# Spins in any idle bank, the first layer by weight block, weight sums at a later rank, two additions of the last tile on ScalarE and GpSimd

## The chip, the core and the metric

The program runs on one NeuronCore of a Trainium2 chip. The metric is the device time of one execution in microseconds, the median of three runs. The engines are TensorE (PE; its weight loads are listed as PEld), VectorE (DVE), ScalarE (ACT), GpSimd (POOL) and SyncE (SP), which issues nearly all DMA transfers.

## The reference

Attention with random features over 8 batches, 8 heads, 576 positions and 64 columns a head, and behind it a normalised two-layer network on the 4608 joined rows of 512:

```
proj = einsum('bhsd,md->bhsm', x, omega); h = proj - sum(x*x)/2
phi  = exp(h - max(h)) / sqrt(m)
kv = einsum('bhsm,bhsd->bhmd', phi(k), v); z = sum(phi(k))
attn = (phi(q) @ kv) / (phi(q) . z + 1e-6)
x   = attn as (B, S, H*D)
xn  = (x - mean) / sqrt(var + 1e-6) * g_ln
out = x + relu(xn @ w_ch1) @ w_ch2
```

`w_ch1` is 512 x 2048 and `w_ch2` 2048 x 512.

## The kernel before

The 4608 rows are nine tiles of 512 (`NT`), each of four chunks of 128 rows (`TC`). For each tile the kernel makes features of queries and keys, the sums `kv` of keys and values, the quotient `x`, its transposition `xnT`, the first layer (`mm1`, or `seven` from tile 2 on, with fewer products and more additions) and the second layer (`mm2`, or `deep` for the last two tiles). Float32 products are made of three products of a rounded high part and a low part.

The order on every engine is written by a planner in the kernel (`Plan`): each generator says which engine it will occupy and for how long by the planner's own figures, waits for keys (`wait`) or takes buffers and PSUM banks by name (`get`), and the planner picks what is ready first, by rank. PE, DVE, ACT, POOL and SP each execute their instructions in that order. Between engines, and from one tile to the next in the same buffer, the framework puts waits on semaphores: a new tile in a bank waits for the last writer and the readers of the tile before it.

In the first 39 us there is no layer to run yet. Chunks of keys are multiplied with `omega` (L909), DVE takes the maximum (L766), ACT the exponential (L784, or L772 on DVE and L778 on ACT for the chunks in `WIDE`), and PE multiplies with the values into `kv` (L827). Queries go through L957, a copy (L259 on ACT), a maximum over partitions on POOL (L1024), L1027 on DVE and L1032 on ACT; L1099 is their product with `kv`, L1111 to L1121 the quotient, L1148 and L1150 mean and variance, L1262 the centring, L1397 the transposition by PE, L1400 and L1402 its high and low part. Beside these, the weights are unpacked and split on DVE and ACT (L418 to L453; L446 is the last part of a first-layer block).

Times in which PE would have nothing are filled with spins (L370), matmuls of a constant of 256 columns that nobody reads. They all write one tile, `pw`, in the eighth bank, `banks[-1]`, which nothing else may use until the first layer starts. `gen_warm` issues them one by one at the rank for idle time, `sums` and `products` one after each group.

The first layer of tile 0 starts in `opening` for the four blocks of 128 columns `f` and for two halves `j` of the rows; it waits for the four weight blocks `w1_0` to `w1_3`, for two chunks of `xnT`, and runs `f` outside and `k` (the weight block) inside. `gen_sides` makes sums of first-layer weights that `seven` needs from tile 2 on. At the end, `combined` adds the partial sums of the last tile (L1847), and `quadrant` adds each quarter, scaled, to `x` (L1903) on DVE; when both quarters of a chunk are done, SP stores it (L1913).

## Time and profile before

| | us |
|---|---|
| median of 3 runs (909.53 to 909.95) | 909.66 |
| the profiled execution | 909.5 |
| its span, first to last instruction | 907.7 |
| PE busy | 902.0 |
| DVE busy | 777.1 |
| ACT busy | 543.2 |
| POOL busy | 138.2 |

The rows that are cited later come from four views. The page gives the busy time of each engine. The view by windows gives it for a stretch, with the count of instructions in brackets and the granted clock of TensorE. The timeline gives instructions in order of time: start, time, engine, line, operation, tile written and tiles read, count; in square brackets what the engine waited for ahead of it. A merged row of several instructions runs from the first one's start to the last one's end, so a step between two is the time less the length of one, divided by the count less one. The view by lines gives the mean length of one instruction. In the chain of waits a row is a stretch of the chain that ended last.

### The profile page before, as it was taken

To read this page: it belongs to the slowest core of one execution; us is meant where nothing else is said; L and a number is where in the kernel's file an instruction comes from. 1 tells how busy PE (TensorE), PEld (TensorE's weight loads), DVE (VectorE), ACT (ScalarE), POOL (GpSimd) and SP (SyncE) were. 2 spreads that over 40 slices of the span, in tenths; PEclk is the share of its full clock that TensorE was granted. 3 is DMA by queue.
4 is the path that set the end of the run, shared out by engine and by line. 5 is a ranking of instruction groups with operands and counts; after the bars stand their busy time and mean duration, and the time that the engine had idled before them with its cause. 6 is when DMAs were issued, how large, how long until landed. Compare 5 with 4: busy or idle time off the path is not lost.

```text
span 907.7 us, 21830 instructions
## 1 busy us (share of the span) xinstructions
PE 902.0 (99%) x8159; PEld 822.2 (91%) x8159; DVE 777.1 (86%) x1799; ACT 543.2 (60%) x1303; POOL 138.2 (15%) x107
## 2 busy tenths in 40 slices
PE   9999999999999999999999999999999999999998
PEld 7888788888899999998999999999999999999998
DVE  6999988989888899779898998888878788778767
ACT  7988876546566477546774666556555553453442
POOL 4201503300112042000220131002301400000000
PEclk9999999999999999999999999999999999999999
DMA  9199665558898898988999988889777869998981
GB/s 349 70 352 363 242 201 173 150 146 261 291 349 287 281 366 270 307 296 288 299 338 310 329 278 273 307 296 357 233 230 237 292 180 325 374 318 295 360 293 48
DMA packets 153146, 249.92 MB, mean 275 GB/s; under 512 B 13264, under 2 KB 66640, under 8 KB 153040
## 3 DMA queue, kind: packets, MB, share of 16 engines
q1 hardware_dynamic: 152752, 248.45, 81.2%
q8 instruction: 65, 1.06, 0.5%
q14 instruction: 41, 0.34, 0.1%
q10 hardware_dynamic: 288, 0.07, 0.0%
HBM read 205.47 MB, written 42.99 MB: 274 GB/s over the span
## 4 chain that ended last, share of the span: by engine, by line
PE 96%; DVE 2%; DMA 1%; ACT 0%; issue 0%; ACTq 0%; DVEq 0%
PE b L1421 38%; PE b L1510 29%; PE b L1794 7%; PE b L1759 6%; PE b L827 4%; PE b L1187 4%; PE b L865 2%; PE b L909 2%; PE b L1448 1%; PE b L370 1%; PE b L957 1%; PE b L1099 1%; DVE v L1847 0%; DVE kp L1903 0%; DMA hid<-omT 0%; DMA w<-side 0%
## 5 line engine op out<-in xcount | busy, mean ns | idle before, releaser
L1421 PE MATMUL b<-w,hid 128*128 128x512 f32 x1090 | 261.9, 385 | 0.0
L1421 PEld LDWEIGHTS b<-w,hid 128*128 128x128 f32 x1090 | 198.9, 188 | 34.0 <-issue 0.3
L1024 POOL PARTITION_ALL_REDUCE wide<-wide x72 | 134.8, 1893 | 473.8 <-ACT wide L259 271.4
L1510 PE MATMUL b<-xnT,w 128*128 128x256 f32 x1344 | 174.0, 276 | 0.0
L1510 PEld LDWEIGHTS b<-xnT,w 128*128 128x128 f32 x1344 | 164.3, 188 | 2.8
L1510 PE MATMUL b<-w,w 128*128 128x256 f32 x1008 | 126.1, 276 | 0.0
L1574 DVE TENSOR_TENSOR w<-b,w 128x256 f32<-128x256 f32 x224 | 108.7, 485 | 15.9 <-PE b L1510 10.4
L1510 PEld LDWEIGHTS b<-w,w 128*128 128x128 f32 x1008 | 120.5, 188 | 1.5 <-DVE w L1574 0.3
L880 ACT ACTIVATE kp<-kp,mb 128x128 f32<-128x128 f32 x184 | 66.9, 397 | 34.0 <-DVE mb L877 33.7
L1421 PE MATMUL b<-xnT,w 128*128 128x512 f32 x324 | 79.4, 387 | 0.0
L1421 PEld LDWEIGHTS b<-xnT,w 128*128 128x128 f32 x324 | 59.7, 187 | 12.0 <-issue 1.0
L1032 ACT ACTIVATE wide<-wide 128x512 f32<-128x512 f32 x72 | 45.4, 635 | 37.7 <-DVE wide L1027 37.7
L1759 PE MATMUL b<-w,hid 128*128 128x256 f32 x460 | 64.4, 279 | 0.0
L1759 PEld LDWEIGHTS b<-w,hid 128*128 128x128 f32 x460 | 57.6, 188 | 1.4
L1600 ACT ACTIVATE hid<-w 128x256 fp32r<-128x256 f32 x85 | 40.4, 513 | 30.4 <-DVE w L1574 24.7
L259 ACT COPY wide<-b 128x512 f32<-128x512 f32 x69 | 39.4, 586 | 28.5 <-PE b L1421 20.0
L1794 PE MATMUL b<-w,wide 128*128 128x256 f32 x408 | 52.4, 275 | 0.0
L1602 DVE SCALAR_TENSOR_TENSOR hid<-w,hid 128x256 fp32r<-128x256 f32 x85 | 48.3, 586 | 4.1 <-ACT hid L1600 3.3
L1027 DVE TENSOR_TENSOR wide<-wide,wide 128x512 f32<-128x512 f32 x64 | 47.0, 743 | 3.6 <-POOL wide L1024 3.4
L986 DVE TENSOR_TENSOR wide<-wide,wide 64x512 fp32r<-64x512 f32 x56 | 40.8, 734 | 9.7 <-ACT wide L984 8.2
L1794 PEld LDWEIGHTS b<-w,wide 128*128 128x128 f32 x408 | 49.1, 188 | 0.0
L886 ACT COPY kp<-b 128x256 f32<-128x256 f32 x92 | 31.4, 368 | 24.0 <-PE b L865 23.8
(171 smaller groups left out, 1453.6 us busy)
## 6 DMA issues: line engine op xcount, KB each, us to landing
w<-side SPq DMA_DIRECT2D x224, 256.0 KB, 5.0
w<-kept SPq DMA_DIRECT2D x80, 512.0 KB, 5.2
w<-kept SPq DMA_DIRECT2D x67, 256.0 KB, 5.2
w<-w SPq DMA_DIRECT2D x32, 512.0 KB, 7.2
wide<-qD SPq DMA_DIRECT2D x56, 256.0 KB, 5.3
w<-deep SPq DMA_DIRECT2D x47, 256.0 KB, 5.5
wide<-kD SPq DMA_DIRECT2D x40, 256.0 KB, 5.1
kept<-w SPq DMA_DIRECT2D x16, 512.0 KB, 3.9
```

The costliest lines, as they stand in the source:

```text
L880: nc.scalar.activation(out=kp[:, j], in_=kp[:, j], func=AF.Exp, scale=1.0, bias=mb[:, j : j + 1])
L986: nc.vector.tensor_tensor(out=qs[D:P], in0=qraw[D:P], in1=f32(qs[D:P]), op=ALU.subtract)
L1024: nc.gpsimd.partition_all_reduce(mx, qc, P, bass_isa.ReduceOp.max)
L1027: nc.vector.tensor_tensor(out=qc, in0=pq if direct else qc, in1=mx, op=ALU.subtract)
L1032: nc.scalar.activation(out=qc, in_=qc, func=AF.Exp)
L1421: nc.tensor.matmul(out.rearrange(f"p ({lies}) -> {order}", a=AW, b=BW), lhsT, rhs.rearrange(f"p (a c b) -> {order}", a=AW, b=BW), start=st ...
L1510: nc.tensor.matmul(passes(out), left(k, l), passes(right[:, r, k]), start=start and k + l + r == 0, stop=k + r == 2, skip_group_check=True,)
L1574: nc.vector.tensor_tensor(out=out, in0=left, in1=right, op=ALU.add)
L1600: nc.scalar.activation(out=hl[:, 0, cols], in_=x, func=AF.Relu)
L1602: nc.vector.scalar_tensor_tensor(out=hl[:, 1, cols], in0=x, scalar=0.0, in1=f32(hl[:, 0, cols]), op0=ALU.max, op1=ALU.subtract)
L1759: nc.tensor.matmul(accs[i].rearrange("p (c a b) -> p c a b", a=AW, b=BW)[:, :, n * 8 : n * 8 + 8], hl[:, l, cs], w[:, r, n * HC : (n + 1) ...
L1794: nc.tensor.matmul(out.rearrange("p (c a b) -> p c a b", a=8, b=8), left[:, l, chunk * P : (chunk + 1) * P], right[:, r].rearrange("p (a c ...
```

## The change

`warm` no longer writes one tile: it takes, of all banks that the planner knows to be free by then, the one free longest, and makes a new tile in it; the eighth bank is no longer set aside. The copies of query features of the first two blocks may go to DVE too. `opening` waits for each weight block when it comes to it, and for the first half of the rows runs `k` outside and `f` inside; `mm1` waits block by block too. In the last tile, the quarter `n == 1` of chunks 2 and 3 is scaled on ACT and added on GpSimd. The rank of the weight sums grows by 12 a group where it grew by 1. Of the two wide chunks of keys, the second is now chunk 3. Since the planner works from these figures, the order of many instructions in the layers differs.

```
-    pw = tile_of(banks[-1], [P, 512], F32, ps)[:, 0 : 2 * P]
-
-    def warm(n):
-        if not mlp_on:
+    def warm(n, at=0.0):
+        idle = [] if mlp_on else [x for x in banks if plan.places.get(x, 1e9) <= plan.cur.end - at]
+        if n and idle:
+            to = bank(min(idle, key=plan.places.get), 2 * P)
             for _ in range(n):
-                nc.tensor.matmul(pw, spin[:, 0:P], spin, start=True, stop=True)
+                nc.tensor.matmul(to, spin[:, 0:P], spin, start=True, stop=True)
...
-        eng = yield "run", {ACT: 0.48, DVE: 0.62} if blk >= T // QB else {ACT: 0.58}
+        eng = yield "run", {ACT: 0.48, DVE: 0.62} if blk >= T // QB else {ACT: 0.58, DVE: 0.62}
...
-        for k in range(NK):
-            yield wait("w", 1, k)
...
-            for f in range(count):
+            places = [(k, f) for k in range(NK) for f in range(count)]
+            for k, f in places if j == 0 else sorted(places, key=lambda x: x[1]):
                 if j == 0:
+                    yield wait("w", 1, k)
+                if j == k == 0:
...
     def mm1(t, f):
-        for k in range(NK):
-            yield wait("w", 1, f // NK * NK + k)
...
         for k in range(NK):
+            yield wait("w", 1, f // NK * NK + k)
             yield us(PE, 3 * 0.225)
...
+        acc = acc.rearrange("p (c r) -> p c r", r=P // 2)
+        if t == NT - 1 and i >= 2 and n == 1:
+            yield act(HC)
+            nc.scalar.activation(out=acc, in_=acc, func=AF.Copy, scale=rss[:, c : c + 1])
+            yield us(POOL, 0.8)
+            nc.gpsimd.tensor_tensor(out=half, in0=acc, in1=half, op=ALU.add)
+        else:
+            yield dve(HC)
...
     def gen_warm():
-        plan.places.pop(banks[-1])
         plan.cur.after = 1.0
         while not mlp_on:
             cold = plan.cur.end < COLD
-            yield us(PE, 0.29 if cold else 0.11)
-            warm(1)
+            cost = 0.29 if cold else 0.11
+            yield us(PE, cost)
+            warm(1, cost)
             plan.cur.after = plan.cur.end + (0.0 if cold else WARM)
-        free(banks[-1])
...
-            plan.add(RSIDE + g, gen_sides(g, k))
+            plan.add(RSIDE + 12 * g, gen_sides(g, k))
...
-WIDE = ((0, 0), (0, 2))
+WIDE = ((0, 0), (0, 3))
```

On PE, at the start of the program, in the kernel before: the last two of thirteen spins and the first product of keys (`om`). A name is a bank, `b0` to `b7`, with the number of the tile in it; the words in brackets are the semaphores that the instruction waits for.

```order
L370 LDWEIGHTS spin_74
L370 MATMUL b7_93<-spin_74 128x256
L370 LDWEIGHTS spin_74
L370 MATMUL b7_93<-spin_74 128x256
L909 MATMUL b0_136<-om_86,w2_150_95 128x128 [waits DMAHW1_49,DVE_49]
L909 MATMUL b1_137<-om_86,w2_150_95 128x128
```

The same place on PE in the changed kernel.

```order
L370 MATMUL b0_135<-spin_74 128x256 [waits PE_49]
L370 LDWEIGHTS spin_74
L370 MATMUL b6_139<-spin_74 128x256
L370 LDWEIGHTS spin_74
L370 MATMUL b6_141<-spin_74 128x256 [waits PE_49]
L370 LDWEIGHTS spin_74
L370 MATMUL b6_143<-spin_74 128x256 [waits PE_49]
L370 LDWEIGHTS spin_74
L370 MATMUL b6_145<-spin_74 128x256 [waits PE_49]
L909 MATMUL b0_148<-om_86,w2_150_94 128x128 [waits DMAHW1_49,DVE_49]
L909 MATMUL b1_149<-om_86,w2_150_94 128x128
```

Spins that shared one tile now have a tile each, and each that takes the bank of the spin before it waits for PE's own semaphore. The program has 101 spins before and 64 now; 45 of the 64 wait for the matmul directly ahead of them.

On PE, where the first layer starts, in the kernel before: the last of ten spins, the third transposition (`ident`), and the first layer (`xnT`, `w1_0` with the number 369, `w1_1`).

```order
L370 LDWEIGHTS spin_74
L370 MATMUL b7_93<-spin_74 128x256
L1397 MATMUL b5_712<-ident_76,wide10_693 128x128 [waits PE_49,Activation_49]
L1397 MATMUL b5_712<-ident_76,wide10_693 128x128 x3
L1448 MATMUL b6_710<-xnT0_624,w1_00_369 128x4x8x8 [waits DVE_49,PE_49]
L1448 MATMUL b6_710<-xnT0_624,w1_00_369 128x4x8x8
L1448 MATMUL b6_710<-xnT0_624,w1_00_369 128x4x8x8 [waits DVE_49]
L1448 MATMUL b6_710<-xnT0_624,w1_10_493 128x4x8x8 x3
```

The same place in the changed kernel, behind nine spins.

```order
L370 MATMUL b6_719<-spin_74 128x256 [waits PE_49]
L370 LDWEIGHTS spin_74
L370 MATMUL b6_721<-spin_74 128x256 [waits PE_49]
L1448 MATMUL b6_724<-xnT0_627,w1_00_452 128x4x8x8 [waits PE_49,Activation_49]
L1448 MATMUL b6_724<-xnT0_627,w1_00_452 128x4x8x8
L1448 MATMUL b6_724<-xnT0_627,w1_00_452 128x4x8x8 [waits DVE_49]
L1448 MATMUL b4_734<-xnT0_627,w1_00_452 128x4x8x8 x3
L1448 MATMUL b2_739<-xnT0_627,w1_00_452 128x4x8x8 x3
L1448 MATMUL b3_743<-xnT0_627,w1_00_452 128x4x8x8 x3
L1448 MATMUL b6_724<-xnT0_627,w1_10_517 128x4x8x8 x3
```

The third transposition has moved behind the first two weight blocks, and the first block now serves four banks in a row. Ahead of this place the spin groups of 17, 10 and 10 have become 18, 8 and 9.

On DVE, at the end of the program, in the kernel before: the last sums (L1847) and the additions to `x` (`kp`, L1903).

```order
L1847 TENSOR_TENSOR v2_12379<-v0_12378,b4_11555 128x512 [waits DVE_49]
L1847 TENSOR_TENSOR v0_12378<-v0_12378,b0_11536 128x512 [waits DVE_49]
L1903 SCALAR_TENSOR_TENSOR kp1_9416<-v2_12379,rss_83,kp1_9416 128x4x64
L1847 TENSOR_TENSOR v1_12380<-v1_12380,b7_11611 128x512 [waits PE_49]
L1903 SCALAR_TENSOR_TENSOR kp1_9416<-v2_12379,rss_83,kp1_9416 128x4x64
L1903 SCALAR_TENSOR_TENSOR kp1_9416<-v0_12378,rss_83,kp1_9416 128x4x64 [waits DVE_49]
L1903 SCALAR_TENSOR_TENSOR kp1_9416<-v0_12378,rss_83,kp1_9416 128x4x64
L1903 SCALAR_TENSOR_TENSOR kp0_9415<-b3_3342,rss_83,kp0_9415 128x4x64 [waits PE_49]
L1903 SCALAR_TENSOR_TENSOR kp0_9415<-v1_12380,rss_83,kp0_9415 128x4x64 [waits DVE_49]
L1903 SCALAR_TENSOR_TENSOR kp0_9415<-v1_12380,rss_83,kp0_9415 128x4x64
L1903 SCALAR_TENSOR_TENSOR kp0_9415<-b2_3343,rss_83,kp0_9415 128x4x64 [waits PE_49]
```

The same place on DVE in the changed kernel.

```order
L1846 TENSOR_TENSOR v2_12462<-v0_12461,b4_11638 128x512 [waits DVE_49]
L1846 TENSOR_TENSOR v0_12461<-v0_12461,b0_11619 128x512 [waits DVE_49]
L1846 TENSOR_TENSOR v1_12463<-v1_12463,b7_11694 128x512 [waits PE_49]
L1909 SCALAR_TENSOR_TENSOR kp1_9499<-v0_12461,rss_83,kp1_9499 128x4x64 [waits DVE_49]
L1909 SCALAR_TENSOR_TENSOR kp1_9499<-v0_12461,rss_83,kp1_9499 128x4x64
L1909 SCALAR_TENSOR_TENSOR kp0_9498<-b2_3475,rss_83,kp0_9498 128x4x64 [waits PE_49]
L1909 SCALAR_TENSOR_TENSOR kp0_9498<-v1_12463,rss_83,kp0_9498 128x4x64 [waits DVE_49]
L1909 SCALAR_TENSOR_TENSOR kp0_9498<-v1_12463,rss_83,kp0_9498 128x4x64
L1909 SCALAR_TENSOR_TENSOR kp0_9498<-b3_3476,rss_83,kp0_9498 128x4x64 [waits PE_49]
```

The two additions from `v2` have left DVE; they are the last two instructions on POOL, behind two scalings that are the last two on ACT. The stores on SP keep their order, chunks 2, 3, 0, 1, and the first two also wait for POOL.

## Rows read from the trace of the kernel before

**Rows 1.** The page, busy time, share and instructions of each engine.

```profile
PE 902.0 (99%) x8159; PEld 822.2 (91%) x8159; DVE 777.1 (86%) x1799; ACT 543.2 (60%) x1303; POOL 138.2 (15%) x107
```

**Rows 2.** Windows: stretch, us, busy of PE PEld DVE ACT POOL, PEclk, DMA, GB/s.

```profile
6.11:21.31 15.20, 15.11 (x235) 12.07 (x231) 13.86 (x31) 13.48 (x35) 9.28 (x6) 1.00 1.04 398
...
38.98:903.66 864.68, 864.58 (x7617) 792.62 (x7615) 744.47 (x1720) 512.73 (x1224) 122.28 (x91) 1.00 0.83 277
```

**Rows 3.** Timeline of the start: start, us, engine, line, operation, tiles, count, wait.

```profile
1.19 2.95 PE L370 MATMUL b<-spin 128*128 128x256 bf16 x13 [1.19 <-DVE spin L330]
...
4.22 1.66 PEld L909 LDWEIGHTS b<-om,w 64*128 64x128 f32 x16 [0.56 <-DVE om L376]
...
6.11 1.29 DVE L766 TENSOR_REDUCE mb<-b 128x4 f32<-128x512 f32 x2 [1.94 <-PE b L909]
```

**Rows 4.** By lines, until 4.1 us and from 9 to 38.3: busy us, mean ns.

```profile
L370 PE MATMUL b<-spin 128*128 128x256 bf16 x13 | 3.0, 419 | 1.2 <-DVE spin L330 1.2
...
L370 PE MATMUL b<-spin 128*128 128x256 bf16 x88 | 13.2, 275 | 0.0
```

**Rows 5.** Timeline of PE from the first L1099 to the first L1448.

```profile
26.95 0.69 PE L1099 MATMUL b<-kv,wide 128*64 128x65 f32 x16
...
30.06 2.03 PE L370 MATMUL b<-spin 128*128 128x256 bf16 x17
...
35.57 1.27 PE L370 MATMUL b<-spin 128*128 128x256 bf16 x10
...
37.11 1.25 PE L370 MATMUL b<-spin 128*128 128x256 bf16 x10
38.57 0.66 PE L1397 MATMUL b<-ident,wide 128*128 128x128 f32 x4 [0.21 <-ACT wide L1262]
38.98 2.64 PE L1448 MATMUL b<-xnT,w 128*128 128x256 f32 x21
```

**Rows 6.** Timeline of DVE, three neighbours late in the program.

```profile
892.87 0.43 DVE L1664 SCALAR_TENSOR_TENSOR kv<-w 128x256 f32<-128x256 f32 x1
893.33 0.43 DVE L1677 TENSOR_TENSOR kv<-kv 128x256 f32<-128x256 f32 x1
893.67 0.42 DVE L1602 SCALAR_TENSOR_TENSOR hid<-w,hid 128x256 fp32r<-128x256 f32 x1
```

**Rows 7.** Timeline of DVE and ACT around the last keys of the first batch.

```profile
18.11 0.68 DVE L434 SCALAR_TENSOR_TENSOR wide<-w 128x512 uint32<-128x512 uint32 x1
...
20.02 1.29 DVE L766 TENSOR_REDUCE mb<-b 128x4 f32<-128x512 f32 x2 [0.50 <-PE b L909]
...
20.74 2.17 ACT L784 ACTIVATE w<-b,mb 128x128 f32<-128x128 f32 x8 [0.43 <-DVE mb L766]
```

**Rows 8.** The chain of waits around 210 us: start, us, what.

```profile
210.37 25.11 PE b L1421 x114
...
250.71 2.73 PE b L1510 x24
```

**Rows 9.** Timeline of the last 11 us: DVE, PE and SP's queue.

```profile
897.15 3.63 DVE L1847 TENSOR_TENSOR v<-v,b 128x512 f32<-128x512 f32 x5
...
903.16 0.50 PE L1794 MATMUL b<-w,hid 128*128 128x256 f32 x3
903.27 0.87 DVE L1903 SCALAR_TENSOR_TENSOR kp<-v,rss,kp 128x256 f32<-128x256 f32 x2
904.06 0.48 DVE L1903 SCALAR_TENSOR_TENSOR kp<-b,rss,kp 128x256 f32<-128x256 f32 x1
```

**Rows 10.** Timeline of POOL, two reductions over partitions.

```profile
12.48 3.77 POOL L1024 PARTITION_ALL_REDUCE wide<-wide  x2 [1.28 <-ACT wide L259]
```

**Rows 11.** Timeline at the second group of first-layer blocks: DVE and PE.

```profile
57.93 0.75 DVE L446 SCALAR_TENSOR_TENSOR w<-wide,g_sb,w 128x512 fp32r<-128x512 f32 x1
...
58.38 2.80 PE L1421 MATMUL b<-xnT,w 128*128 128x512 f32 x12
```

More of the change, by code (lines that the diff above doesn't have):

```diff
@@ L1443, in opening @@
                 cs = slice(f % 2 * P, (f % 2 + 1) * P)
-                for k in range(NK):
-                    yield us(PE, 3 * 0.1134)
-                    w = wparts[1, k][:, f // 2]
-                    for l, r in ((0, 0), (1, 0), (0, 1)):
-                        nc.tensor.matmul(
-                            out, w[:, l, cs],
-                            passes(xnT[:, r, k])[:, :, 8 * j : 8 * j + 8],
-                            start=j + k + l + r == 0, stop=j == 1 and k == NK - 1 and r == 1, skip_group_check=True,
-                        )
-                if j == 1:
+                yield us(PE, 3 * 0.1134)
+                w = wparts[1, k][:, f // 2]
+                for l, r in ((0, 0), (1, 0), (0, 1)):
+                    nc.tensor.matmul(
+                        out, w[:, l, cs],
+                        passes(xnT[:, r, k])[:, :, 8 * j : 8 * j + 8],
+                        start=j + k + l + r == 0, stop=j == 1 and k == NK - 1 and r == 1, skip_group_check=True,
+                    )
+                if j == 1 and k == NK - 1:
                     done(("mm1", 0, f))
@@ L1459, in mm1 @@
     def mm1(t, f):
-        for k in range(NK):
-            yield wait("w", 1, f // NK * NK + k)
         for i in range(TC):
@@ L1900, in quadrant @@
             yield wait("part", t, i, None)
-        yield dve(HC)
         half = x.rearrange("p (c n r) -> p n c r", n=2, r=P // 2)[:, n or 0]
-        nc.vector.scalar_tensor_tensor(
-            out=half, in0=acc.rearrange("p (c r) -> p c r", r=P // 2), scalar=rss[:, c : c + 1], in1=half,
-            op0=ALU.mult, op1=ALU.add,
-        )
+        acc = acc.rearrange("p (c r) -> p c r", r=P // 2)
[6 more added lines that the diff above has]
+            yield dve(HC)
+            nc.vector.scalar_tensor_tensor(
+                out=half, in0=acc, scalar=rss[:, c : c + 1], in1=half, op0=ALU.mult, op1=ALU.add
+            )
         done(("part", t, i, n))
```

## The prediction

> **What bounds the kernel now.** I read the page first: PE is busy for 902.0 of 907.7 us [rows 1]. Then the windows: from the first layer's first matmul at 38.98 us to the last at 903.66 PE is busy for 864.58 of 864.68 us [rows 2], so no wait of PE worth naming is left there. For the same matmuls the end can only move with two things: when the first layer starts, and the tail from PE's last matmul to the last store, 907.7 - 903.66 = 4.0 us. The rest of the argument is about the first 39 us, where PE executes in program order, real products and spins (L370) mixed, each spin group filling a time in which data is made ready by DVE, ACT and GpSimd. The profiled execution took 909.5 us (span 907.7); the median of the three runs is 909.66, so I add the sum to 909.66.
>
> **What a spin costs, before and after.** The first thirteen spins take 2.95 us [rows 3] and last 0.419 us each [rows 4]: a step of (2.95 - 0.42)/12 = 0.211 us for 256 columns, the 1.2 GHz level. Later a spin lasts 0.275 us [rows 4], and seventeen take 2.03 us [rows 5]: a step of (2.03 - 0.28)/16 = 0.110 us, the 2.4 GHz level. Step is shorter than length because spins overlap: they all write one tile, b7, and none waits. In the changed order each spin gets a tile of its own, and one that lands in the bank of the spin just before it carries a wait on PE's own semaphore, which that spin raises at its end. I count 47 waits on the directly preceding matmul where the kernel before has none, 45 of them on spins. Such spins can't overlap: the step becomes length plus signal. No row shows this on PE. The nearest are on DVE [rows 6]: two neighbours without such a wait start 0.34 us apart (893.67 after 893.33), while the operation that waits for the one just before it starts 0.46 us after it, which is its length of 0.43 plus 0.03. So I take 0.275 + 0.03 = 0.305 us a spin, and 0.42 + 0.03 = 0.45 at the low clock. The lower end is the old 0.110, if the wait costs nothing.
>
> **The change, part by part.**
> (1) *First spins.* Thirteen stay, eleven with a wait. The thirteenth starts at 1.19 + 11 x 0.45 + 0.21 = 6.35 us and the first product of keys behind it at 6.56, where it now starts at 4.22, on om [rows 3]: +2.3 us, and the first reduction on DVE (6.11 now) goes with it. If the clock also rises later, two product groups cost up to half the 1.66 us of the first group's loads [rows 3] more each: bounds 0 and +4.0.
> (2) *Work up to the first L1099.* Eight banks instead of seven, the WIDE chunk moved, copies allowed on DVE. Between the first and the last of the ten reductions DVE has in the new order four weight operations fewer (L426, L430, L434, L267; at most 0.68 us each, [rows 7]) and one copy more: three fewer, at 0.4 to 0.68, about -1.6. DVE is busy for 13.86 of 15.20 us there [rows 2]; of the 1.34 us idle I give half back, -0.7. From the end of the last exponentials (20.74 + 2.17 = 22.91, [rows 7]) to the first L1099 at 26.95 [rows 5] 4.0 us pass, with twelve spins and a product of queries among the work; the new order has two L827 groups of about 0.63 us, five spins (4 x 0.305 + 0.11 = 1.33) and the copies of the sums: about 3.4, so -0.6. Together -2.9, bounds -1.2 and -4.8. With (1), the first L1099 comes at 26.95 + 2.3 - 2.9 = 26.35.
> (3) *From the first L1099 to the first L1448.* Now 38.98 - 26.95 = 12.03 us [rows 5]. The real products are the same but for the third transposition. The spin groups change: 17 at 0.11 = 1.9 become 18, sixteen of them waiting: 16 x 0.305 + 0.22 = 5.1 (+3.2). Ten, 1.1, become eight, six waiting: 2.05 (+0.95). Ten become nine, eight waiting: 2.55 (+1.45). Away go PE's wait in front of the third transposition (37.11 + 1.1 = 38.21 to 38.57, -0.36) and the transposition (38.57 to 38.98, -0.41). Sum +4.8; with a signal between nothing and 0.06 us, +3.9 to +5.7. I take the sum whole, because the data that these groups cover is ready before they end: a transposition's copy and the next centring on ACT are some 1.3 us, less than the new groups behind it.
> (4) *First layer by weight block.* Its 96 matmuls stay, in another order. It removes the wait for w1_3, whose last part now stands behind the second L1402 on DVE; I cost it at nothing, since PE arrives later than before. The third transposition returns inside it: +0.41.
> (5) *Weight sums put off, new order of the layers.* Same instructions on DVE and SP. PE has 43 matmuls of 512 columns fewer and 86 of 256 more: 86 x 2.73/24 - 43 x 25.11/114 = +0.3 [rows 8]. New waits: bounded by nothing and 1 us; I take nothing, because PE has none now [rows 2], and the weights get the time by which the layer starts later.
> (6) *The tail.* PE ends at 903.66 (903.16 + 0.50), but the last addition on DVE starts at 904.06, behind two others from 903.27 [rows 9]. Two quarter additions (some 0.4 us each) leave DVE, so the last starts at about 903.70: -0.36. Their scaling on ACT and addition on GpSimd begin when the fourth L1847 ends: 897.15 + 3 x 0.74 + 0.68 = 900.05. The stores wait on SP in order; the two of the chunks that GpSimd adds stand first, so a late GpSimd holds back the last store too. No row has a GpSimd addition; the nearest is its reduction over 128x512, 3.77/2 = 1.89 us [rows 10]: at that price the second addition ends at 900.05 + 0.5 + 3.8 = 904.3 and the last store is some 0.8 us later than now. Bounds -0.36 and +0.8; I take -0.36, since the operands here have half the elements and no exchange between partitions. The Trainium skill (GPSIMD Engine Reference, 3.1 Elementwise) has 4497 ns for an addition of 2048 elements; an estimate from it is 0.56 us here, which would leave -0.36 too.
>
> Sum: (1) +2.3, (2) -2.9, (3) +4.8, (4) +0.4, (5) +0.3, (6) -0.36 = +4.55. 909.66 + 4.55 = **914.2 us**. With the bounds of (1) to (3) partly offsetting each other: 911.5 to 917.
>
> **Rivals.**
> *A wait on PE's own semaphore costs nothing* (the spins keep 0.110). For: in-order PE has no need of the wait, and no row shows one that close. Against: [rows 6]. Then (1) is 0, (2) is -2.9 less another 0.8 for its five spins, (3) is +0.1 - 0.2 - 0.1 - 0.77 = -1.0; with (4) to (6) about -4.3. Of that something is given back: w1_7's last part is ready at 57.93 + 0.75 = 58.68 and needed about nine matmuls of 0.22 after 58.38, at 60.4 [rows 11], a margin of 1.7 us that such a start exceeds, so -2.0 to -4.3: **906.5 us**. This is the faster side. Where it tips: thirty waiting spins behind the first L1099, four ahead of it and eleven slow ones at the start make some 0.45 us for each 0.01 us of step, so from a step of about 0.20 us on the change is slower.
> *The clock falls.* Waiting spins occupy the array for 0.11 of each 0.305 us, for 5 us in the longest group; before that group nothing so thin is seen, and the granted clock is 1.00 in the rows of the windows [rows 2]. If it falls to 1.2 GHz, the fourteen waiting spins after it cost 0.145 more each (2.0 us) and up to 22 of the first layer's matmuls run at half rate (2.3 us): **917 to 918.5 us**. By the Trainium skill (TensorE: Matmul & The Clock Gate, A second HAM failure mode: psum-queue depth-cycling) PE that idles briefly and often while it cycles through banks can swing between its two clock levels; the row shows no such fall in the kernel before, which has no waits of that kind.
> *The spin groups do cost, but the front gains more* (all of DVE's idle time and the low end of (2) and (3)): **910.5 us**.
>
> **Chances.** Forecast 0.60, clock 0.12, smaller loss 0.08, free waits 0.20. The range leaves out the free waits alone: 909.5 to 918. A measurement of this kernel tells 0.2% (1.8 us) from no change: faster 0.18 (the free waits without their slow end), same 0.10 (that end and most of the smaller loss), slower 0.72.
>
> **What would show it.** In the changed kernel's profile: spins in a group of one bank 0.30 us apart (0.11 would prove me wrong at the root); the first L909 at 6.3 to 6.8 us and the first DVE reduction near 8; the first L1099 at 25.5 to 27.5; the first layer's first matmul at 42 to 45 us; PE again without waits from there to its end; the last addition on DVE within 0.1 us of PE's end. A first layer that starts before 38 us, or PE waits of more than 1 us in all behind it, would make the prediction wrong.

## The result, and the profile after

The changed kernel takes 920.39 us (median of six runs, 919.36 to 923.57) against 909.99 us: a ratio of 1.0119 (1.0103 to 1.0135). The forecast was 914.2 us, at most 918. The direction was right; the forecast growth (4.2 us over this median) is less than half of the measured 10.4 us.

The profiled execution is the longest of the six: 923.57 us, span 921.7 us, 14.0 us more than the span before (907.7). The span in four stretches, before and after:

| stretch | before, us | after, us | difference |
|---|---|---|---|
| start to first L1448 | 38.98 | 49.07 | +10.09 |
| first L1448 to first L1421 | 11.45 | 13.48 | +2.03 |
| first L1421 to PE's end | 853.23 | 855.48 | +2.25 |
| PE's end to the end of the span | 4.05 | 3.67 | -0.38 |

The timeline of PE after (start, time, engine, line, operation, tiles, count, and in brackets what PE waited for ahead of it):

```profile
1.17 5.30 PE L370 MATMUL b<-spin 128*128 128x256 bf16 x13 [1.17 <-DVE spin L330]
6.40 2.08 PE L909 MATMUL b<-om,w 64*128 64x128 f32 x16
8.27 1.92 PE L957 MATMUL b<-wide,om 64*128 64x256 f32 x8
...
12.58 1.03 PE L957 MATMUL b<-wide,om 64*128 64x256 f32 x8
...
19.64 1.16 PE L909 MATMUL b<-om,wide 64*128 64x128 f32 x14 [0.93 <-DVE w L727]
...
28.80 0.69 PE L1099 MATMUL b<-kv,wide 128*64 128x65 f32 x16
...
31.91 6.27 PE L370 MATMUL b<-spin 128*128 128x256 bf16 x18
38.11 1.14 PE L1099 MATMUL b<-kv,wide 128*64 128x65 f32 x16
...
43.43 2.34 PE L370 MATMUL b<-spin 128*128 128x256 bf16 x8
...
46.05 2.87 PE L370 MATMUL b<-spin 128*128 128x256 bf16 x9
49.07 4.57 PE L1448 MATMUL b<-xnT,w 128*128 128x256 f32 x24
...
62.55 5.47 PE L1421 MATMUL b<-w,hid 128*128 128x512 f32 x24
```

Read the spins first. Before, seventeen took 2.03 us [rows 5]; now eighteen take 6.27. The nine at 46.05 us take 2.87 us and the last of them lasts 0.28, so a step is (2.87 - 0.28)/8 = 0.324 us (0.325 below) where it was 0.110. Then read the products: L1099 behind the long group takes 1.14 us for sixteen, 0.69 ahead of it. PE itself is slower there. The windows of after (stretch, length, busy time and count of each engine, granted clock, DMA share, GB/s) say so in the clock's column:

```profile
31.91:35.58 3.67, 3.05 (x16) 1.14 (x13) 3.33 (x10) 3.67 (x16) 0.77 (x3) 1.00 0.00 0
35.58:42.41 6.83, 6.55 (x60) 4.09 (x60) 2.08 (x10) 1.77 (x3) 0.00 (x0) 0.50 0.01 2
42.41:49.23 6.82, 5.89 (x42) 2.96 (x41) 4.74 (x13) 5.01 (x17) 0.00 (x0) 1.00 0.00 0
49.23:52.65 3.42, 3.42 (x17) 3.42 (x17) 2.91 (x8) 2.17 (x4) 0.00 (x0) 0.50 0.00 0
...
62.55:918.03 855.48, 854.85 (x7559) 783.17 (x7557) 731.40 (x1704) 503.40 (x1215) 124.18 (x93) 1.00 0.84 279
```

The granted clock is at the lower of its two levels (1.2 GHz) from 35.58 to 42.41 us and again from 49.23 to 52.65, where the first layer begins. Before, it was 1.00 in [rows 2], and between them in the stretch from the first L1099 on:

```profile
26.95:38.98 12.03, 11.82 (x184) 9.65 (x184) 11.78 (x38) 11.16 (x32) 2.58 (x4) 1.00 0.01 3
```

At the very start the column reads 1.00 in both kernels, though the first spins of the kernel before step by 0.211 us and later ones by 0.110. That PE runs there at the lower level is read from the lengths alone: in the changed kernel eight L957 still take 1.92 us at 8.27 us, and 1.03 at 12.58.

The last row of after answers to the second of [rows 2]: in the layers behind the opening PE waits for 0.63 us (855.48 less 854.85) where it waited for 0.10 us before, but they are 2.25 us longer.

The tail went as forecast. DVE's last addition starts 0.10 us behind PE's end (918.03), where it was 0.40 us [rows 9]; ScalarE and GpSimd are done well before:

```profile
914.47 0.91 ACT L1904 ACTIVATE v<-v,rss 128x256 f32<-128x256 f32 x2 [3.77 <-DVE v L1846]
915.07 1.67 POOL L1906 TENSOR_TENSOR kp<-v,kp 128x256 f32<-128x256 f32 x2 [172.38 <-ACT v L1904]
...
918.13 0.47 DVE L1909 SCALAR_TENSOR_TENSOR kp<-b,rss,kp 128x256 f32<-128x256 f32 x1
```

### The profile page after: what moved, and what is told of

The parts are those of the page before. It is cut to its first block, busy times and chain, and to the rows that moved or that the text cites. A ratio compares the mean times of both kernels' runs of the same rounds, so it can differ in the third digit from the quotient of the medians.

```text
span 921.7 us, 21865 instructions
## 1 busy us (share of the span) xinstructions
PE 911.9 (99%) x8165; PEld 825.0 (90%) x8165; DVE 775.8 (84%) x1799; ACT 544.8 (59%) x1317; POOL 141.1 (15%) x109
## 4 chain that ended last, share of the span: by engine, by line
PE 91%; DVE 5%; DMA 2%; ACT 1%; issue 1%; DVEq 0%; SPq 0%
PE b L1421 35%; PE b L1509 28%; PE b L1793 7%; PE b L1758 6%; PE b L1187 4%; PE b L827 3%; PE b L865 2%; PE b L1448 1%; DMA w<-w 1%; PE b L370 1%; PE b L909 1%; PE b L1479 1%; PE b L1099 1%; DMA w<-kept 1%; DVE w L1573 0%
## 5 line engine op out<-in xcount | busy, mean ns | idle before, releaser
L1421 PE MATMUL b<-w,hid 128*128 128x512 f32 x1065 | 254.2, 384 | 0.0
L1421 PEld LDWEIGHTS b<-w,hid 128*128 128x128 f32 x1065 | 194.7, 188 | 33.3 <-issue 0.3
L1509 PEld LDWEIGHTS b<-xnT,w 128*128 128x128 f32 x1344 | 165.1, 188 | 3.3
L1421 PE MATMUL b<-xnT,w 128*128 128x512 f32 x306 | 76.5, 389 | 0.0
L1758 PE MATMUL b<-w,hid 128*128 128x256 f32 x510 | 69.6, 278 | 0.0
L1032 ACT ACTIVATE wide<-wide 128x512 f32<-128x512 f32 x72 | 45.8, 636 | 35.5 <-DVE wide L1027 34.0
L1421 PEld LDWEIGHTS b<-xnT,w 128*128 128x128 f32 x306 | 56.0, 187 | 11.4 <-issue 1.0
L1254 ACT ACTIVATE wide<-x,mvs 128x512 f32<-128x512 f32 x28 | 35.0, 1260 | 16.0 <-DVE mvs L1150 7.0
L986 DVE TENSOR_TENSOR wide<-wide,wide 64x512 fp32r<-64x512 f32 x56 | 38.6, 700 | 5.6 <-ACT wide L984 4.2
```

What stands on the lines that cost most here:

```text
L986: nc.vector.tensor_tensor(out=qs[D:P], in0=qraw[D:P], in1=f32(qs[D:P]), op=ALU.subtract)
L1032: nc.scalar.activation(out=qc, in_=qc, func=AF.Exp)
L1421: nc.tensor.matmul(out.rearrange(f"p ({lies}) -> {order}", a=AW, b=BW), lhsT, rhs.rearrange(f"p (a c b) -> {order}", a=AW, b=BW), start=st ...
L1509: nc.tensor.matmul(passes(out), left(k, l), passes(right[:, r, k]), start=start and k + l + r == 0, stop=k + r == 2, skip_group_check=True,)
L1758: nc.tensor.matmul(accs[i].rearrange("p (c a b) -> p c a b", a=AW, b=BW)[:, :, n * 8 : n * 8 + 8], hl[:, l, cs], w[:, r, n * HC : (n + 1) ...
```

## The experiments

Fourteen kernels, in three questions: is it the spins' waits, through what do they cost, and what do the other edits do? "Ratio" is always against the kernel before on the same chip. Line numbers of some kernels are shifted by up to six (L1453 or L1444 for L1448 and so on).

### Is it the waits?

The first kernel takes the changed one and lets spins share a tile as long as nothing else used the bank.

```
-            to = bank(min(idle, key=plan.places.get), 2 * P)
+            name = min(idle, key=plan.places.get)
+            if spun[0] != (name, plan.places[name]):
+                spun[:] = (name, plan.places[name]), bank(name, 2 * P)
+            to = spun[1]
```

> The changed kernel, and only the tiles of the spins differ: a spin takes the tile of the spin before it as long as it is in the same bank and nothing else used the bank in between, so none of the 64 spins waits for PE's own semaphore; the order on every engine is that of the changed kernel, row for row. Theory A (the waits of the spins, and the clock that they cost): the step of two spins goes from 0.325 us to 0.15 us, the first product of keys starts near 4.2 us, the clock is granted in full near 6 us instead of 11.7 us, no later stretch is at half of it, the first L1448 starts at 36 to 39 us (49.07 with the waits), and the time is 905 to 909 us. Theory B (the order of the other work, made by the planner, is what costs; the spins follow it): 916 to 921 us. Theory C (64 spins are too few where 101 stood before, waits or not): the clock still falls in the front, and the time is 910 to 916 us.

Measured: 911.59 us, ratio 1.0015 (1.0006 to 1.0024). The waits alone, with every row of the order the same, are worth 8.8 us of the 10.4 by the medians (9.4 by the ratios). Theory A holds, but the end is 2.6 us above its range: the front comes out as it said, the rest does not. Its timeline of PE:

```profile
1.17 2.96 PE L375 MATMUL b<-spin 128*128 128x256 bf16 x13 [1.17 <-DVE spin L330]
4.25 1.28 PE L914 MATMUL b<-om,w 64*128 64x128 f32 x16
...
10.38 0.69 PE L832 MATMUL b<-w,kp 128*64 128x65 f32 x16 [0.95 <-ACT kp L789]
...
16.90 1.16 PE L914 MATMUL b<-om,wide 64*128 64x128 f32 x14 [0.93 <-DVE w L732]
...
25.20 0.69 PE L1104 MATMUL b<-kv,wide 128*64 128x65 f32 x16
...
28.31 1.48 PE L375 MATMUL b<-spin 128*128 128x256 bf16 x12
30.29 0.81 PE L375 MATMUL b<-spin 128*128 128x256 bf16 x6 [0.49 <-DVE wide L1032]
...
36.16 1.15 PE L375 MATMUL b<-spin 128*128 128x256 bf16 x9
37.46 3.06 PE L1453 MATMUL b<-xnT,w 128*128 128x256 f32 x24
```

Nine spins take 1.15 us again, a step of (1.15 - 0.28)/8 = 0.109 us. The first L1448 (here L1453) starts at 37.46 us, 11.6 us ahead of the changed kernel.

The second does the reverse: the kernel before, with a tile for each call of the spins.

```
-    pw = tile_of(banks[-1], [P, 512], F32, ps)[:, 0 : 2 * P]
...
+            pw = bank(banks[-1], 2 * P)
```

> The kernel before, and only the tiles of the spins differ: each call of the spins makes a tile of its own in the reserved eighth bank, so nearly every one of the 101 spins waits for the matmul ahead of it; the order on every engine stays that of the kernel before. Theory A (waits and clock): the first product of keys starts near 6.4 us (4.22 without), the clock is granted in full later than 5.7 us, the first L1448 starts at 43 to 50 us (38.98 without), and the time is 914 to 921 us. Theory B (the order costs, not the waits): the waits are hidden, 909 to 911 us. Between them, 911 to 914 us, the waits would cost their own length in the front and the clock nothing.

Measured: 929.00 us, ratio 1.0205 (1.0191 to 1.0219), 8 us beyond the range of theory A. Not a row of the order differs, so 19 us are the price of the waits on PE's own semaphore, with what the clock loses by them:

```profile
1.19 5.52 PE L369 MATMUL b<-spin 128*128 128x256 bf16 x13 [1.19 <-DVE spin L330]
6.64 2.08 PE L908 MATMUL b<-om,w 64*128 64x128 f32 x16
...
41.35 5.51 PE L369 MATMUL b<-spin 128*128 128x256 bf16 x17
46.79 0.95 PE L1098 MATMUL b<-kv,wide 128*64 128x65 f32 x16
...
58.62 2.65 PE L1447 MATMUL b<-xnT,w 128*128 128x256 f32 x21
```

The seventeen spins take 5.51 us, (5.51 - 0.28)/16 = 0.327 us a step, where they took 2.03; 0.217 us more each. At 1.2 GHz the first thirteen step by (5.52 - 0.42)/12 = 0.425 us against 0.211 before [rows 3]. There are 86 spins in seven groups of ten and more, so 79 such steps; 79 x 0.217 = 17.1 us. The front is 58.62 - 38.98 = 19.6 us longer. The rest fits two stretches with a low clock:

```profile
30.30:33.59 3.29, 3.29 (x42) 2.18 (x42) 0.46 (x1) 1.07 (x2) 0.50 (x1) 0.53 0.00 0
46.79:50.46 3.67, 3.67 (x52) 2.86 (x51) 2.21 (x8) 0.93 (x4) 0.00 (x0) 0.54 0.02 4
```

The same instructions took 1.91 us (22.78 to 24.69) and 2.40 us (32.02 to 34.42) before, 2.65 us less. Behind the first L1421 the two are alike, 853.12 us (70.04 to 923.16) against 853.23.

The third undoes the spins' edit and keeps all others; the planner makes a new order.

```
-    def warm(n, at=0.0):
-        idle = [] if mlp_on else [x for x in banks if plan.places.get(x, 1e9) <= plan.cur.end - at]
...
+    pw = tile_of(banks[-1], [P, 512], F32, ps)[:, 0 : 2 * P]
```

> The changed kernel with the first of its edits undone: the spins write one tile in the eighth bank again, which is set aside until the first layer starts (109 spins, none with a wait on PE). All other edits stay, and the planner makes its order anew. Theory A (waits and clock of the spins): within 3 us of the kernel before, 906 to 911 us. Theory B (the other edits, by the order that they make): 915 to 921 us.

Measured: 912.87 us, ratio 1.0032 (1.0020 to 1.0044). Far nearer to A's 906 to 911 than to B's 915 to 921, but 1.9 us above: the other edits cost some 3 us without the waits.

### Which waits, and through what?

Each spin in the next idle bank in turn, so that it waits for a matmul two or more back:

```
-            to = bank(min(idle, key=plan.places.get), 2 * P)
+            spun[0] += 1
+            to = bank(idle[spun[0] % len(idle)], 2 * P)
```

> The changed kernel, and only the banks of the spins differ: each spin makes a tile of its own as there, but in the next of the idle banks in turn instead of the one free longest; the order of the instructions on every engine is that of the changed kernel. 37 of the 64 spins still wait for PE, but most of these for a matmul two or more back, and some spins now wait for a reader of their bank on DVE or ScalarE. Theory A (it is the wait for the matmul directly ahead that makes the step of 0.325 us): the step in the first group is 0.12 to 0.17 us again, the first L1448 starts at 37 to 41 us, and the time is 910 to 914 us, near the kernel with shared tiles (911.6 us). Theory B (any wait for PE's own semaphore costs the same): steps of 0.3 us stay where the wait is for PE, the first L1448 starts at 43 to 49 us, 915 to 921 us. Theory C: a spin that waits for DVE or ScalarE holds back the work queued behind it, over 921 us.

Measured: 912.88 us, ratio 1.0030 (1.0019 to 1.0041). Theory A. Two groups in one timeline:

```profile
24.84 1.57 PE L373 MATMUL b<-spin 128*128 128x256 bf16 x5 [0.22 <-DVE wide L1030]
...
29.68 2.89 PE L373 MATMUL b<-spin 128*128 128x256 bf16 x18
```

Five spins that had one bank alone to go to step by (1.57 - 0.28)/4 = 0.32 us; eighteen that go round several by (2.89 - 0.28)/17 = 0.154. It is the wait for the matmul directly ahead that costs.

The changed kernel without any spin (`warm` returns at once), and the kernel before without any:

> The changed kernel without any spin: the 64 spins are left out (nobody reads what they write), and the order of all else is the same. No spin waits and none fills the gaps. Theory A (in the changed kernel the length of the waiting spins is the larger loss, 9.5 of the 11.6 us that the front is longer than with shared tiles, and the clock that they hold or lose the smaller): shorter than the changed kernel though the clock is at half of its rate for most of the front, 913 to 919 us. Theory B (the clock is the larger loss): as long as the changed kernel or longer, 920 to 930 us. In both the first product of keys starts before 4 us, as soon as its data are there.

> The kernel before without its 101 spins, which nobody reads; the order of all else on every engine is the same. Theory A (a spin that does not wait is nearly free and buys the full clock in the front; without it the clock's half rate costs the front about what the empty places give back, as in the changed kernel without spins, 912.88 us against 911.59 us with shared tiles): 911 to 914 us, the granted clock under 0.8 somewhere between 20 and 45 us. Theory B (the spins that stand ahead of ready work are themselves a loss in the kernel before): 907 to 909.5 us.

Measured: 912.88 us (ratio 1.0029, 1.0018 to 1.0040) for the first, just below its expected range, and 911.38 us (1.0020, 1.0011 to 1.0030) for the second, inside theory A. No spins at all are 7.5 us better than spins that wait, though the clock falls. The kernel without spins, timeline and windows:

```profile
31.31 1.03 PE L1095 MATMUL b<-kv,wide 128*64 128x65 f32 x28 [0.99 <-ACT wide L1028]
...
37.89 5.57 PE L1444 MATMUL b<-xnT,w 128*128 128x256 f32 x24 [0.68 <-ACT xnT L1396]
```

```profile
25.24:37.89 12.65, 7.40 (x136) 5.96 (x136) 11.72 (x36) 11.25 (x31) 4.95 (x5) 0.80 0.04 13
37.89:52.36 14.47, 14.47 (x104) 14.24 (x105) 13.07 (x25) 12.73 (x29) 0.00 (x0) 0.82 0.27 87
```

The first L1448 (here L1444) starts at 37.89 us, because PE there waits for DVE and ScalarE anyway. The half clock is paid in the opening: 14.47 us against 12.13 with shared tiles. So spins that don't wait are worth 2 us or less, and the waits took more than that.

Last, between no wait and 45: the rule for sharing with at most two, and at most four, spins a tile (22 and 10 waits).

```
-            if spun[0] != (name, plan.places[name]):
+            if spun[0] != (name, plan.places[name]) or spun[2] == 2:
```

> The changed kernel, and only the tiles of the spins differ: two spins in a row share a tile where nothing else used the bank between them, then the next two. 22 spins wait for the matmul directly ahead, where the changed kernel has 45 and the one with shared tiles none; the order on every engine is the same in the three. Theory A (the loss is the length of the waits, 0.216 us each, from steps of 0.325 against 0.109 us): the first L1448 starts near 37.46 + 22 x 0.216 = 42.2 us, and the time is in proportion between 911.6 and 920.4 us, 915 to 917 us. Theory B (the loss comes with the fall of the clock and not with the waits): either no half-rate stretch behind 15 us and 911 to 913.5 us, or such stretches and 918 to 921 us.

> As the kernel with two spins a tile, with up to four: 10 spins wait for the matmul directly ahead. Theory A (proportion): the first L1448 starts near 37.46 + 10 x 0.216 = 39.6 us, 913 to 914.5 us. Theory B (the clock's fall, not the waits): 911 to 912.5 us, as with shared tiles, as long as the clock stays.

Measured: two a tile 913.71 us, ratio 1.0045 (1.0028 to 1.0061); four a tile 911.54 us, ratio 1.0023 (1.0012 to 1.0033). By ratios, so many per cent of 910 us, the kernels lie 1.4 (no wait), 2.1 (10), 4.1 (22) and 10.8 us (45) above the kernel before. Neither theory is right as put: it is not in proportion (that would be 3.5 and 6.0), and not all or nothing: four a tile lies in the range of B, two a tile 0.2 us above it. Against B as the cause of the loss speaks that two a tile is 2.7 us behind no wait with the clock at 1.00 behind 26 us, and that one of the six runs of the changed kernel has a mean granted clock of 1.000 and takes 919.36 us. With two a tile the clock stays:

```profile
29.19 3.87 PE L376 MATMUL b<-spin 128*128 128x256 bf16 x18
...
40.67 2.97 PE L1454 MATMUL b<-xnT,w 128*128 128x256 f32 x24
```

```profile
26.07:40.67 14.60, 13.60 (x177) 9.01 (x178) 12.62 (x38) 12.07 (x37) 4.31 (x4) 1.00 0.02 5
```

Its 22 waits are 22 x 0.216 = 4.75 us of PE's time, but the first layer starts only 40.67 - 37.46 = 3.2 us later: 1.5 us lie in time that PE would have waited anyway, such as the 0.49 us ahead of L1032's data in the kernel with shared tiles. The next 23 waits are 5.0 us more, and the front grows by 49.07 - 40.67 = 8.4. The 3.4 us above that go to the clock by its rows: L1099 and its neighbours from 38.11 to 42.15 us in the changed kernel take 4.04 us at half rate, the same rows before 2.40 (32.02 to 34.42), +1.6; the first products up to the first sums 7.4 us (6.40 to 13.81) against 6.4 with two a tile (5.12 to 11.52), +1.0; and the end of the long group (35.58 to 38.11 us), an estimate of six spins at 0.425 instead of 0.325 us, +0.6.

### The other edits

The tail alone, in the kernel before (its rows on PE and SP do not move):

```
+        if t == NT - 1 and i >= 2 and n == 1:
+            yield act(HC)
+            nc.scalar.activation(out=acc, in_=acc, func=AF.Copy, scale=rss[:, c : c + 1])
+            yield us(POOL, 0.8)
+            nc.gpsimd.tensor_tensor(out=half, in0=acc, in1=half, op=ALU.add)
```

> The kernel before with one edit of the change alone: the quarter n == 1 of chunks 2 and 3 of the last tile is scaled on ScalarE and added on GpSimd. Nothing else moves. The forecast's term: the last addition on DVE starts within 0.1 us of the end of PE instead of 0.11 to 0.4 us behind, and 0.36 us less, 909.6 us against 909.99 us. Rival: the end is set by the store's transfer and not by the addition, 0.0 us. Rival: the addition on GpSimd ends later than the one on DVE would, +0.8 us at most.

Measured: 910.39 us, ratio 0.9999 (0.9990 to 1.0008). The expected 0.4 parts in a thousand lie inside the interval, so the time doesn't tell. The trace does: PE ends at 905.03 us and the span at 908.7, 3.7 us where it was 4.05.

The opening alone; the rank of the sums alone; the wide chunk and the copies alone; each in the kernel before:

```
+            for k, f in places if j == 0 else sorted(places, key=lambda x: x[1]):
...
-            plan.add(RSIDE + g, gen_sides(g, k))
+            plan.add(RSIDE + 12 * g, gen_sides(g, k))
...
-WIDE = ((0, 0), (0, 2))
+WIDE = ((0, 0), (0, 3))
```

> The kernel before with one edit of the change alone: the first layer begun by weight block, with its waits block by block. The planner makes its order anew. The forecast's own price for this edit is +0.4 us for the third transposition, within 0.2 us of the kernel before otherwise. Theory A (the edit by itself is nearly free): 909.8 to 911 us. Theory B (any new order of the layers costs 1.5 to 4 us, as in the five kernels with a new order so far, whose time from the first block of 512 columns on was 854.4 to 857.1 us against 852.96): 911 to 914 us.

> The kernel before with one edit of the change alone: the rank of the weight sums at 12 a group instead of 1. Front and opening stay (first L1448 at 38.98 us). The forecast's price: +0.3 us, 910.3 us. Theory A (a new order of the layers costs 1.5 to 4 us in stalls and transitions, whichever edit makes it): 911.5 to 914 us. Theory B (this edit shortens: fewer sums where DVE is wanted): 908 to 909.5 us.

> The kernel before with the two smallest edits alone: chunk 3 of the keys instead of chunk 2 is a wide one, and the copies of query features of the first two blocks may go to DVE. The forecast put them into the earlier first L1099 (2.9 us of it by all edits together). Theory A (the front gains from them): the first L1099 is before 26.5 us (26.95 before). Theory B (they put more work on DVE in the front): it is later than 27 us, as in the changed kernel with reserved spins, 27.59 us. In both the layers have a new order, so the time is 910 to 914 us.

Measured: 912.60 us (ratio 1.0031, 1.0020 to 1.0042), 925.08 us (1.0171, 1.0156 to 1.0186) and 919.84 us (1.0114, 1.0089 to 1.0139). The opening is free in itself: it lasts 11.43 us (39.22 to 50.65) against 11.45, and the loss is all behind it, 856.49 us against 853.23. The other two went beyond what either theory gave, and the wide chunk doesn't help the front either (first L1099 at 27.48 us, as theory B has it). Before, PE waits 0.10 us in all of the layers [rows 2]; with the rank of the sums alone it waits 7.5 us there, of 14.6 us by which they are longer, and with the wide chunk and the copies alone 6.1 us of 10.7. The rank of the sums alone has these waits among others, two at the features of a later tile and one where L1794 begins:

```profile
452.02 0.50 PE L1421 MATMUL b<-wide,om_hi 128*128 128x512 f32 x1 [0.84 <-ACT wide L259]
...
455.01 0.79 PE L1421 MATMUL b<-wide,om_hi 128*128 128x512 f32 x1 [2.25 <-DVE wide L986]
...
772.88 0.92 PE L1794 MATMUL b<-x,wide 128*128 128x256 f32 x6 [2.33 <-issue]
```

Two more, to find what makes the layers longer: the kernel with shared tiles and the old rank of the sums, and the kernel before with shared tiles in idle banks alone.

```
-        plan.add(RSIDE + 12 * g, gen_sides(g, k))
+        plan.add(RSIDE + g, gen_sides(g, k))
```

> The kernel with shared tiles of the spins (e1_share, 911.59 us), and the rank of the weight sums back to RSIDE + g. The front up to the first L1448 is as in e1_share (37.46 us). Theory A (the later rank of the sums is what makes the layers 2.2 us longer there, by 43 blocks of 512 columns turned into 86 of 256 and by stalls of PE at 261, 330 and 432 us): 907.5 to 910 us, PE has no stall over 0.15 us but the one that the kernel before has near 462 us. Theory B (another edit, or the shifted start, makes the order in the layers worse, whatever the rank): 911 to 913 us.

```
-    pw = tile_of(banks[-1], [P, 512], F32, ps)[:, 0 : 2 * P]
...
+            if spun[0] != (name, plan.places[name]):
+                spun[:] = (name, plan.places[name]), bank(name, 2 * P)
```

> The kernel before with the first edit of the change alone, but without its cost: spins in any idle bank, with the tile shared as long as nothing else used the bank (76 spins, none waits for PE), and the eighth bank no longer set aside. The planner makes its order anew. Theory A (the freed bank lets the front start earlier, 1.5 us in e1_share, and it is the other edits that lengthen the layers): the first L1448 starts at 37 to 38.5 us, and the time is 908 to 910 us. Theory B (any new order in the front moves the layers' order by one to three microseconds either way, and the front's gain does not show): 910 to 913 us.

Measured: 914.25 us (ratio 1.0041, 1.0026 to 1.0056) and 913.71 us (1.0044, 1.0027 to 1.0061). Both start the first layer early, at 37.36 and 38.12 us, and lose it again. Theory A falls in both, and they are a microsecond above the range of B. From the first L1421 to PE's end:

| kernel | first L1448, us | first L1421 to PE's end, us |
|---|---|---|
| before | 38.98 | 853.23 |
| before, tile for each spin | 58.62 | 853.12 |
| before, tail alone | 39.52 | 854.07 |
| before, no spins | 39.43 | 853.40 |
| changed | 49.07 | 855.48 |
| changed, shared tiles | 37.46 | 855.42 |
| changed, reserved bank | 41.23 | 855.52 |
| shared tiles, old rank of the sums | 37.36 | 857.07 |
| before, shared tiles in idle banks | 38.12 | 857.35 |
| before, opening alone | 39.22 | 856.49 |
| before, rank of the sums alone | 39.29 | 867.82 |
| before, wide chunk and copies alone | 41.47 | 863.95 |
| changed, banks in turn | 38.88 | 857.25 |
| changed, no spins | 37.89 | 854.68 |
| changed, two spins a tile | 40.67 | 855.58 |
| changed, four spins a tile | 40.84 | 855.10 |

Every new order is longer than that of before, by 1.5 us and up to 14.6. The order isn't all. The first four rows have the order of before on PE and lie between 853.12 and 854.07 us; the changed kernel, the one with shared tiles and the last four rows have the changed order and lie between 854.68 and 857.25. The two ranges don't meet, but within the second there are 2.6 us that the order doesn't explain, one profiled execution each; the runs don't tell what does. In the kernel with shared tiles two of its waits are plain, again at the features of a later tile:

```profile
330.42 0.49 PE L1426 MATMUL b<-wide,om_hi 128*128 128x512 f32 x1 [0.18 <-DVE kp L893]
...
433.13 0.50 PE L1426 MATMUL b<-wide,om_hi 128*128 128x512 f32 x1 [0.39 <-DVE kp L893]
```

With the changed mix of 256 and 512 columns (+0.3 us by the forecast's reckoning) that makes 0.9 of the 2.2 us; the rest is spread over many short steps between matmuls, and I have no single cause for it.

## Why the prediction was wrong

The predicted sum was +4.55 us, the profiled execution shows 923.57 - 909.5 = 14.1; its spans differ by 14.0. Of the 9.4 us that the sum lacks, term (3) makes 3.4, (2) 2.6, (5) 2.0 and (4) 1.6. Part of (2), (3) and (4) is a lower clock, which the sum left to a rival. The clock alone did not put the forecast out: the run with a mean granted clock of 1.000 takes 919.36 us, above the range too, and the kernel with shared tiles, at 1.00, misses the forecast's own terms by 1.95 us in (2) and 1.9 us in (5). So the steps that failed whatever the clock are (2), which took the front's data to come earlier, and (5), which took the layers to stay as they were. Step by step:

- *The step of a waiting spin*, the root of the forecast: right. 0.305 us was taken, 0.325 is measured (0.45 against 0.425 at the low clock). The kernel with shared tiles and the one with waits added to the kernel before show that the waits make most of the loss. The rival of free waits falls.
- *Term (1), first spins*, +2.3 us: right. The first L909 starts at 6.40 instead of 4.22, +2.2.
- *Term (2), the work up to the first L1099*, -2.9 us: failed; it measures -0.3 (22.40 us from the first L909 against 22.73). The first L1099 was to come at 26.35 us and comes at 28.80. With shared tiles it comes at 25.20, 1.75 us ahead of the kernel before, where the forecast's own terms would have given 23.3 (26.95 - 2.9 - 0.8). The estimate counted DVE's operations and took half of its idle time back; but in the new order PE waits for data where it waited for nothing before: 2.56 us in five places with shared tiles, 0.95 us for the first exponentials and 0.93 us for L727 (line 732 there) among them; in the changed kernel, where PE comes later, 1.35 us are left of it. The other part is the lower level at the start, held for longer; the bound of (1) had that, its value did not.
- *Term (3), from there to the first L1448*, +4.8 us: mis-sized. 20.27 us (28.80 to 49.07) against 12.03, +8.2. The long group takes 6.20 us instead of 5.1, the last two 5.2 instead of 4.6, and the products between them 1.64 us more at half rate, which the term left to a rival.
- *Term (4), the opening*, +0.41: the edit is free and the transposition returns, as with shared tiles (12.13 us against 11.45, with two transpositions in it for one). The changed kernel has 1.35 us more, at the low clock from 49.23 to 52.65 us.
- *Term (5), sums and order of the layers*, +0.3: failed. It is +2.25, and +2.2 with shared tiles. I took nothing for new waits because PE had none before and the weights got more time. That reason is about when the weights come; the two waits that can be named, 0.57 us, are for the features of later tiles. The rest of the 2 us stays open. The rank of the sums alone would have cost 15 us in the old order. A new order by a planner is not priced by the count of its instructions; the bound of 1 us had no row behind it.
- *Term (6), the tail*, -0.36: right in the trace, -0.38, and GpSimd's two additions take 0.84 us each, near the low price; in the time it can't be told.

The rival that came true in part is the clock. It was priced at 2.0 + 2.3 us for a fall behind the long group, and its place was right: the clock fell inside this group. But it had a chance of 0.12 and a rule that pointed to it. By the Trainium skill (TensorE: Matmul & The Clock Gate, A second HAM failure mode: psum-queue depth-cycling) PE that idles briefly and often can swing between its two levels; the windows of the profiled run agree, 0.50 and 1.00 in turn. Its price was sound for this part of the fall (1.64 + 1.35 us, and some 0.6 us for the long group's last spins), and it left out the slow start.

So the 8.8 us of the waits are mostly their length, 45 x 0.216 = 9.7 us, of which some 1.5 us hide; in the profiled run, which is longer than the median by 3.2 us, the clock adds some 5 us. The other runs separate them in part: at a mean granted clock of 1.000 the time is 919.36 us, at 0.998 it is 919.5 and 919.8, at 0.994 it is 921.2 and 923.57. So about 1 us of the median goes with these falls, and 9.4 us over the kernel before are there without them. Since the clock's column does not show the lower level at the start, this says nothing of the slow start.

No kernel here beats the kernel before. The nearest with a new order is the changed one with shared tiles, 0.15% behind it.

## What to carry to other kernels

Before an instruction that only fills time is given a buffer of its own, ask what it then waits for: a matmul that waits for the matmul directly ahead of it takes its whole length, here three times its step, and a filler on the critical engine that waits is worse than none. Let fillers share one tile, or go round several. And where a planner orders everything, an edit's price is its order's price: measure one edit at a time, and don't add them (three of the edits here cost 2.9, 15.4 and 10.1 us singly, and 2.8 together, with the tail).

## What was not expected of the hardware

- The full step of a dependent matmul: 0.325 us at 2.4 GHz and 0.425 at 1.2 GHz for 256 columns, against 0.109 and 0.211; the difference, 0.216 and 0.214 us, hardly depends on the clock. The Trainium skill (TensorE: Matmul & The Clock Gate, Single matmul latency) gives (398 + N)/2.4 ns for one matmul alone, an estimate of 0.273 us here; the rows have 0.28 us, and 0.045 us more pass before the next one starts. The profile models the ends of matmuls, so the 0.28 is no measurement of its own; the step of 0.325 us is.
- In the profiled run of the changed kernel PE lost the full clock within a group of 18 spins, nearly all at a step of 0.325 us; a group of as many that alternate between 0.325 and 0.109 us kept it. It is not so each time: one run of the changed kernel has a mean granted clock of 1.000, and in the kernel before with a tile for each spin the clock is 1.00 all through its group of 17 (41.35 to 46.79 us) and falls behind it.
- A wait of PE near the start, and 1.2 GHz behind it: in the profiled run with four spins a tile (913.38 us, its longest) PE waits 1.45 us, and the sixteen products behind it take 2.75 us where 1.16 is usual; that fits its first L1448 at 40.84 us, while its median is that of shared tiles. In the kernel with banks in turn PE waits 1.09 us there, and from 14 to 19 us the clock reads 0.66. The timeline of the kernel with four spins a tile, and the window behind the wait with the clock at 0.52:

```profile
13.05 0.69 PE L833 MATMUL b<-w,kp 128*64 128x65 f32 x16 [1.45 <-DVE wide L1033]
13.67 0.34 PE L376 MATMUL b<-spin 128*128 128x256 bf16 x1
14.07 2.75 PE L915 MATMUL b<-om,w 64*128 64x128 f32 x16
```

```profile
14.07:20.91 6.84, 6.78 (x66) 5.84 (x66) 6.83 (x14) 4.94 (x13) 3.91 (x2) 0.52 1.02 403
```

- Waits that nothing in the profile releases: 2.33 us with the rank of the sums alone and 3.28 us with the wide chunk alone, both at the first L1794, where the other kernels have none. PE's queue for weight loads sits in one semaphore wait for 4.45 and 5.40 us until then, where the kernel before has 0.05 us at this line, so it waits for another engine or a transfer; the profile does not name which.
